# Attention and a two-layer network on one core: one 32-byte tile moves from behind the weights to ahead of them

## The chip, the cores and the metric

The kernel runs on one core of a Trainium2 chip. The metric is the device time of one execution in microseconds (us). The profile is of one execution, taken by the hardware profiler. TensorE (PE) multiplies matrices, and its weight loads are listed apart as PEld; VectorE is DVE, ScalarE is ACT, GpSimd is POOL, and SyncE (SP) issues the DMAs.

## What is computed

Attention with a block-causal mask (blocks of 64) over 8 batches, 8 heads, 576 positions and a head size of 64; then a network on the 4608 tokens of 512 features:

```python
scores = scale * np.matmul(q, k.transpose(0, 1, 3, 2))
scores = np.where(block_i >= block_j, scores, -1e9)
attn = softmax(scores)
x = np.matmul(attn, v)            # heads side by side: 4608 x 512
h = x @ w_in                      # 512 x 2048
g = np.maximum(0.01 * h, h)
out = g @ w_out                   # 2048 x 512
```

The large products are taken in a 4-byte type (fp32r). To keep precision, each operand of the large products is split into a high and a low part, and three of the four partial products are summed.

## The kernel before

**Order of the work.** Nothing is scheduled by hand. Each step is handed to a planner (class Plan) with the engines that may do it, a rank and a cost in ns; the planner plays the engines through and writes out one fixed order. Its costs depend on sizes alone, not on addresses.

**Stages.** The weights come in as 64-bit numbers, in 64 pieces, and are turned into high and low parts (wih, wil, woh, wol) during the first part of the run. Batches 0 and 1 go through attention with TensorE transposes, the later ones with VectorE transposes and a way through DRAM (line 703, line 720). As soon as 256 tokens of attention output are there (a chunk; 18 in all), the network runs on them, interleaved with the attention of later heads.

**The first product** (line 805). For each pair of 128-wide columns of w_in, twelve multiplications go into one accumulator of p_h: four slices of the 512 features, and for each the terms xh by wih, xl by wih and xh by wil. The stationary operand (the weight load) is a 128x128 block of wih or wil, 512 bytes per partition; the moving operand is 256 columns of xh or xl, 1024 bytes per partition.

**The second product** (line 824). After the activation (line 812) and its split into gh and gl, six multiplications go into each of two accumulators p_o. Here the stationary operand is a 128x128 block of gh or gl, and the moving operand is 512 columns of woh or wol, 2048 bytes per partition. Over the run there are 288 groups of twelve into p_h, and 288 groups of six into p_o.

**Where tiles lie.** A pool hands out its tiles in the order of their creation, each rounded up to 32 bytes per partition. 384 bytes lie ahead of the first tile (a scratch area of 256 and four constants of 32). The big tiles are whole multiples of 256 bytes, so a tile's place in a 512-byte line follows from what was created before it:

| tiles, in order of creation | bytes per partition, each | byte of the 512-byte line, before |
|---|---|---|
| wih, wil, woh, wol | 32768 | 384 |
| pth | 7168 | 384 |
| prow0_0 to prow0_4 | 512 to 2560 | 384 |
| qk_in0 | 4608 | 384 |
| qs0, qs1, kh0, kh1, kl0, kl1 | 2304 | 384, 128 in turn |
| vs | 2560 | 384 |
| nm0, nm1, sums0, sums1, rec0, rec1 | 32 (20 used) | 384, 416, 448, 480, 0, 32 |
| xr0 | 9216 | 64 |
| g, gh0, gh1, gl0, gl1, xh, xl, ob | 2048 or 4096 | 64 |
| pools of the stages: raw, val, ptf, later xr1, ptl, v_stage, ptm, turn | various | 64 or 320 |

nm holds the negated row maxima of the softmax (line 505 writes, line 514 reads), one small tile for even heads and one for odd ones.

Of the kernel before, what the change touches and what calls it, by code (L numbers as in the profile page):

```python
# [9 lines left out]
F32 = mybir.dt.float32  # L10
# [7 lines left out]
P = 128  # L18
# [3 lines left out]
NT = 5  # L22
# [204 lines left out]
def attention_ffn(ctx: ExitStack, tc: tile.TileContext, qk: bass.AP, v: bass.AP, w_in: bass.AP, w_out: bass.AP, out: bass.AP):  # L227
# [33 lines left out]
    def fixed(shape, dt, name, n=None, pool=const):  # L261
        if n is None:
            return pool.tile(shape, dt, name=name)
        return [pool.tile(shape, dt, name=f"{name}{i}") for i in range(n)]
# [3 lines left out]
    def identity(pool):  # L268
        one = fixed([P, P], F32, "ident", None, pool)
        make_identity(nc, one)  # L270
        return one

    wih = fixed([P, ND, DFF], F32R, "wih")
    wil = fixed([P, ND, DFF], F32R, "wil")
    woh = fixed([P, NF, DM], F32R, "woh")
# [24 lines left out]
    kh = fixed([P, S], F32R, "kh", 2)  # L300
    kl = fixed([P, S], F32R, "kl", 2)
    vs = fixed([P, NT, 2 * D], F32R, "vs")
    nm = fixed([P, NT], F32, "nm", 2)
    sums = fixed([P, NT], F32, "sums", 2)
    rec = fixed([P, NT], F32, "rec", 2)
    for y in range(2):
# [605 lines left out]
```

## Time and profile before

| | |
|---|---|
| median of 3 runs | 1120.84 us (1120.43 to 1126.4) |
| the profiled execution, its own time | 1119.52 us |
| its span, first to last instruction | 1117.7 us |
| TensorE busy, granted clock | 97%, 0.997 |
| weight loads busy | 87% |
| VectorE, ScalarE, GpSimd busy | 68%, 63%, 43% |
| DMA | 148 GB/s over the span |

A row of groups gives line, engine, operation, names, shapes and count, then busy time, the mean of one in ns, and the idle time of the engine before it with what ended it. Multiplications are pipelined: one that is listed with 280 ns is followed by the next after less than half of that, so the pace is read from the starts, or from the chain of waits, which lists pieces as start, length and count.

### The profile page before, as it was taken

Reading aid. Unit: us, or ns where it says so; the run is one execution under the profiler, and the core shown is the slowest. Engines: PE = TensorE matmul, PEld = TensorE weight load, DVE = VectorE, ACT = ScalarE, POOL = GpSimd, SP = SyncE. Lnnn points to the kernel's source line nnn. Section 1 sums busy time; section 2 is a strip of 40 time slices with the busy share of each in tenths; the row PEclk is TensorE's granted clock in tenths of the full one; section 3 lists DMA queues with packets and bytes.
Section 4 is the critical chain, followed back from the end, with each engine's and each line's share of the span. In section 5 each row is a group of like instructions: output and inputs, shape, how many; then the busy total and the mean of one; then the engine's idle time right before and its main releaser. Section 6 shows DMA issues by size and latency. Waiting matters only on the chain.

```text
span 1117.7 us, 20595 instructions
## 1 busy us (share of the span) xinstructions
PE 1083.7 (97%) x6896; PEld 971.3 (87%) x6896; DVE 762.2 (68%) x2115; ACT 708.3 (63%) x1696; POOL 475.5 (43%) x501
## 2 busy tenths in 40 slices
PE   5799999999999999999999999999999999999998
PEld 4578788888889989999999998999989998999997
DVE  6998978879878777877666678787877776400000
ACT  7998767767777766655655566676677765322222
POOL 3444244545544444433443345455444445422221
PEclk9999999999999999999999999999999999999999
DMA  7766421157766656564445456656676655200000
GB/s 235 231 201 198 133 95 61 61 173 208 199 198 189 201 170 201 176 170 147 128 151 148 128 171 185 203 171 203 176 205 185 194 156 160 59 20 19 1 20 19
DMA packets 96810, 166.24 MB, mean 149 GB/s; under 512 B 10176, under 2 KB 79808, under 8 KB 96704
## 3 DMA queue, kind: packets, MB, share of 16 engines
q1 hardware_dynamic: 96704, 164.93, 50.0%
q8 instruction: 54, 0.88, 0.3%
q14 instruction: 52, 0.43, 0.1%
HBM read 111.41 MB, written 53.48 MB: 148 GB/s over the span
## 4 chain that ended last, share of the span: by engine, by line
PE 69%; DVE 16%; ACT 6%; DMA 4%; issue 2%; SPq 1%; POOL 0%; ACTq 0%; DVEq 0%; POOLq 0%
PE p_h L805 27%; PE p_o L824 27%; PE p_t L641 6%; PE p_s L487 6%; DVE nm L505 4%; ACT prow L514 4%; DVE turn L703 2%; DVE qs L464 2%; DMA way<-turn 2%; DMA ptm<-way 2%; PE p_t L568 2%; PE p_s L481 1%; DVE p_s L498 1%; DVE ptl L253 1%; SPq L720 1%
## 5 line engine op out<-in xcount | busy, mean ns | idle before, releaser
L805 PE MATMUL p_h<-xh,wih 128*128 128x256 f32 x1152 | 327.0, 284 | 1.6 <-DVE xh L244 1.6
L805 PE MATMUL p_h<-xl,wih 128*128 128x256 f32 x1152 | 323.1, 280 | 1.0 <-DVE xl L253 0.9
L805 PE MATMUL p_h<-xh,wil 128*128 128x256 f32 x1152 | 322.5, 280 | 0.0
L254 POOL TENSOR_TENSOR gl<-g,gh 128x512 fp32r<-128x512 f32 x110 | 149.4, 1359 | 368.2 <-ACT gh L243 317.7
L805 PEld LDWEIGHTS p_h<-xl,wih 128*128 128x128 f32 x1152 | 218.6, 190 | 11.6 <-DVE xl L253 1.4
L805 PEld LDWEIGHTS p_h<-xh,wih 128*128 128x128 f32 x1152 | 217.9, 189 | 11.8 <-DVE xh L244 1.8
L805 PEld LDWEIGHTS p_h<-xh,wil 128*128 128x128 f32 x1152 | 219.4, 190 | 0.0
L514 ACT ACTIVATE prow<-p_s,nm 128x192 f32<-128x192 f32 (+4 forms) x308 | 160.0, 525 | 74.1 <-DVE nm L505 73.4
L812 ACT ACTIVATE g<-p_h 128x512 f32<-128x512 f32 x144 | 86.0, 597 | 174.6 <-PE p_h L805 168.4
L824 PE MATMUL p_o<-woh,gh 128*128 128x512 f32 x576 | 183.1, 399 | 0.0
L824 PE MATMUL p_o<-wol,gh 128*128 128x512 f32 x576 | 179.7, 393 | 0.0
L824 PE MATMUL p_o<-woh,gl 128*128 128x512 f32 x576 | 179.1, 392 | 0.0
L703 DVE STREAM_TRANSPOSE turn<-prow 128x384 f32<-128x384 f32 (+3 forms) x384 | 143.9, 401 | 33.2 <-POOL prow L542 24.0
L542 POOL TENSOR_SCALAR prow<-prow,rec 128x320 f32<-128x320 f32 (+4 forms) x142 | 77.3, 557 | 148.7 <-DVE rec L529 106.7
L505 DVE TENSOR_REDUCE nm<-p_s 128x1 f32<-128x192 f32 (+4 forms) x308 | 137.4, 480 | 3.3
L824 PEld LDWEIGHTS p_o<-woh,gl 128*128 128x128 f32 x576 | 108.2, 188 | 24.8
L824 PEld LDWEIGHTS p_o<-wol,gh 128*128 128x128 f32 x576 | 108.2, 188 | 24.4
L544 ACT ACTIVATE prow<-prow,rec 128x192 f32<-128x192 f32 (+4 forms) x124 | 75.5, 614 | 48.6 <-DVE rec L529 48.4
L243 ACT CAST gh<-g 128x512 fp32r<-128x512 f32 x139 | 86.1, 620 | 22.0 <-PE p_o L824 20.5
L254 POOL TENSOR_TENSOR ptl<-ptm,pth 128x448 fp32r<-128x448 f32 x83 | 97.6, 1193 | 3.6 <-ACT pth L243 3.6
L243 ACT CAST pth<-ptm 128x448 fp32r<-128x448 f32 x191 | 94.4, 564 | 5.4 <-DMA ptm<-way 4.9
L824 PEld LDWEIGHTS p_o<-woh,gh 128*128 128x128 f32 x576 | 90.9, 188 | 3.6 <-issue 0.4
(81 smaller groups left out, 1655.0 us busy)
## 6 DMA issues: line engine op xcount, KB each, us to landing
way<-turn SPq DMA_DIRECT2D x192, 224.0 KB, 3.0
ptm<-way SPq DMA_DIRECT2D x192, 224.0 KB, 4.3
qk_in<-in_qk SPq DMA_DIRECT2D x56, 576.0 KB, 3.8
v_stage<-in_v SPq DMA_DIRECT2D x56, 160.0 KB, 2.3
out<-ob SPq DMA_DIRECT2D x35, 256.0 KB, 2.5
raw<-in_w_in SPq DMA_DIRECT2D x32, 256.0 KB, 3.3
raw<-in_w_out SPq DMA_DIRECT2D x32, 256.0 KB, 3.4
qk_in<-in_qk SPq DMA_DIRECT2D x8, 320.0 KB, 3.6
```

Of the source, the lines that this page charges most:

```text
L243: one = lambda: nc.scalar.copy(dst(), src())
L254: ("POOL", pool2(n), lambda: nc.gpsimd.tensor_sub(dst(), one(), two())),
L487: go = lambda ap=ap, cols=cols, kk=kk, k0=k0, k1=k1, first=first, last=last: nc.tensor.matmul(ap, qs[z][:, cols], kk[:, k0:k1], start=firs ...
L505: [("DVE", dve(kw[t]), lambda t=t, ap=ap, flat=flat: nc.vector.tensor_reduce(nm[z][: qn[t], t : t + 1], ap[: qn[t]], axis=AX.X if flat els ...
L514: nc.scalar.activation(o, ap[: qn[t]], AF.Exp, bias=nm[z][: qn[t], t : t + 1], scale=1.0, accum_out=sums[z][: qn[t], t : t + 1])
L542: ("POOL", pool1(kw[t]), lambda: nc.gpsimd.tensor_scalar(p(), p(), by, 1.0, op0=ALU.mult, op1=ALU.mult)),
L544: ("ACT", act(kw[t], True), lambda: nc.scalar.mul(p(), p(), by)),
L641: nc.tensor.matmul(to, vs[:, j, :], src, start=start, stop=stop)
L703: nc.vector.transpose(dst, src.rearrange("p (s b i) -> p s b i", b=4, i=32))
L805: nc.tensor.matmul(hh[:, i, :], w[:, d, f * P : (f + 1) * P], x[:, d, :], start=k == 0, stop=k == len(terms) - 1)
L812: add([("ACT", act(512), lambda: nc.scalar.activation(g, hh, AF.Prelu, alpha=0.01))], rank, [("h", z)], ["g"])
L824: nc.tensor.matmul(p_o[m], a[:, i, m * P : (m + 1) * P], w[:, 2 * u + i, :], start=u == 0 and k == 0, stop=u == NU - 1 and k == 5,)
```

## The change

The first of the two small tiles nm is created ahead of the weights and not behind vs. The second is created where both were.

```diff
+    nm = [fixed([P, NT], F32, "nm0")]
     wih = fixed([P, ND, DFF], F32R, "wih")
     wil = fixed([P, ND, DFF], F32R, "wil")
     woh = fixed([P, NF, DM], F32R, "woh")
...
     vs = fixed([P, NT, 2 * D], F32R, "vs")
-    nm = fixed([P, NT], F32, "nm", 2)
+    nm.append(fixed([P, NT], F32, "nm1"))
     sums = fixed([P, NT], F32, "sums", 2)
```

All tiles from wih to vs start 32 bytes further: 384 becomes 416, and 128 becomes 160. nm1 and all that follows it (sums, rec, xr0, g, gh, gl, xh, xl, ob and the stages' pools) stay where they were. The instructions and their order are the same.

## The prediction

> **What bounds the kernel now.** I read the page first, then stretches of the span, then the engine's waits, then the chain of waits.
>
> ```profile
> span 1117.7 us, 20595 instructions
> ...
> PE 1083.7 (97%) x6896; PEld 971.3 (87%) x6896; DVE 762.2 (68%) x2115; ACT 708.3 (63%) x1696; POOL 475.5 (43%) x501
> ...
> PEclk9999999999999999999999999999999999999999
> ```
>
> TensorE is busy for 97% of the span at a granted clock of nine tenths or more in every slice, and apart from its own weight loads no engine comes above 68%. An average hides stages, so I cut the span into stretches; the columns are the stretch, its length, then busy time and instructions of each engine.
>
> ```profile
> 0.00:100.00 100.00, 80.87 (x444) 61.89 (x445) 85.68 (x283) 86.79 (x253) 40.89 (x65) 1.00 0.72 219
> 100.00:400.00 300.00, 289.98 (x1852) 259.20 (x1853) 248.46 (x678) 217.96 (x531) 142.66 (x159) 0.99 0.52 155
> 400.00:800.00 400.00, 399.47 (x2586) 365.26 (x2585) 295.34 (x800) 258.53 (x604) 177.69 (x172) 1.00 0.58 168
> 800.00:1040.00 240.00, 239.49 (x1551) 218.49 (x1550) 130.79 (x355) 126.90 (x282) 97.37 (x92) 1.00 0.42 123
> ```
>
> Up to 100 us TensorE (the first pair of figures) is not the limit: ScalarE and VectorE are each busier. From 400 to 1040 us it is busy for 638.96 of 640 us. The view of waits, TensorE alone, from 400 us to the end, has one row:
>
> ```profile
> PE p_s L487 <- ACT prow L514: 1.0, 4, 0.3
> ```
>
> So for the last 717.7 us TensorE waits 1.0 us in all. There the time is the number of matrix multiplications times the pace at which they follow each other, and nothing else. The multiplications are in these rows (count, busy time, mean of one):
>
> ```profile
> L805 PE MATMUL p_h<-xh,wih 128*128 128x256 f32 x1152 | 327.0, 284 | 1.6 <-DVE xh L244 1.6
> L805 PE MATMUL p_h<-xl,wih 128*128 128x256 f32 x1152 | 323.1, 280 | 1.0 <-DVE xl L253 0.9
> L805 PE MATMUL p_h<-xh,wil 128*128 128x256 f32 x1152 | 322.5, 280 | 0.0
> ...
> L824 PE MATMUL p_o<-woh,gh 128*128 128x512 f32 x576 | 183.1, 399 | 0.0
> L824 PE MATMUL p_o<-wol,gh 128*128 128x512 f32 x576 | 179.7, 393 | 0.0
> L824 PE MATMUL p_o<-woh,gl 128*128 128x512 f32 x576 | 179.1, 392 | 0.0
> ```
>
> 3 x 1152 = 3456 multiplications into p_h are 288 groups of twelve, and 3 x 576 = 1728 into p_o are 288 groups of six. The means of 280 to 399 ns overlap one another, so they are not the pace. The pace is in the chain of waits, whose pieces run from the first start of a group to the first start of the next. From 400 us on its long pieces are:
>
> ```profile
> 747.09 5.54 PE p_o L824 x24
> 753.15 5.65 PE p_h L805 x48
> ...
> 978.85 5.46 PE p_h L805 x48
> 1107.07 6.88 PE p_o L824 x30
> ```
>
> Here is what the case turns on. The same 48 multiplications, of the same shapes from the same tiles, with no wait before any, take 5.65 us at one place and 5.46 us at another: 117.7 against 113.8 ns each. So two paces exist. Short pieces show the mixture, first at 930 us, then at 938 us:
>
> ```profile
> 930.12 1.38 PE p_h L805 x12
> 931.50 1.37 PE p_o L824 x6
> 932.87 1.39 PE p_h L805 x12
> ...
> 938.52 1.41 PE p_h L805 x12
> 939.93 1.39 PE p_o L824 x6
> ```
>
> And inside a group the pace can switch. These are the first, the sixth and the twelfth multiplication of one group, and the first of the next (start, duration):
>
> ```profile
> 1080.67 0.28 PE L805 MATMUL p_h<-xh,wih 128*128 128x256 f32 x1
> ...
> 1081.27 0.28 PE L805 MATMUL p_h<-xh,wil 128*128 128x256 f32 x1
> ...
> 1081.95 0.28 PE L805 MATMUL p_h<-xh,wil 128*128 128x256 f32 x1
> 1082.06 0.62 PE L824 MATMUL p_o<-woh,gh 128*128 128x512 f32 x2
> ```
>
> Five steps in 0.60 us are 120 ns each, the next seven in 0.79 us are 113 ns each. The weight loads run beside the multiplications (PEld, 87%), so two streams leave the on-chip memory at once: the 512 bytes of the next stationary block, and the 1024 or 2048 bytes of the moving operand.
>
> **The change part by part.** No instruction is added, removed or reordered: the planner's costs know no addresses, so the order written out is the same. What changes is where tiles start. Everything allocated between the old and the new place of the small tile moves up by 32 bytes, everything behind it stays. By the tiles' sizes, weights, pth, prow, the first q and k tiles and vs go from byte 384 (or 128) of a 512-byte line to 416 (or 160); xr, g, gh, gl, xh, xl and ob stay at byte 64.
>
> The small tiles themselves cost nothing: the first starts at byte 384 of a line before and after, the second at 416, and the instructions that write and read them are not moved in time.
>
> The loads of q and k land 32 bytes further. They are 3.8 us from issue to landing, and over the run all their readers together idle 1.0 us for them:
>
> ```profile
> qk_in<-in_qk SPq DMA_DIRECT2D x56, 576.0 KB, 3.8
> ...
>   DMA qk_in<-in_qk: 1.0, 3
> ```
>
> The cover is the lead of the load over its use; without it a load slower by a tenth would cost 0.4 us at each of those 3 places. I take 0, between -1 and +1 us.
>
> VectorE, ScalarE and GpSimd read and write moved tiles (prow, qs, kh, kl, vs, pth). The nearest rows compare a subtraction whose three tiles lie at byte 64 with one that mixes 384 with the later pools:
>
> ```profile
> L254 POOL TENSOR_TENSOR gl<-g,gh 128x512 fp32r<-128x512 f32 x110 | 149.4, 1359 | 368.2 <-ACT gh L243 317.7
> ...
> L254 POOL TENSOR_TENSOR ptl<-ptm,pth 128x448 fp32r<-128x448 f32 x83 | 97.6, 1193 | 3.6 <-ACT pth L243 3.6
> ```
>
> 1359 / 512 and 1193 / 448 are 2.65 and 2.66 ns per element: the place does not show. I take 0 here too. The cover from 400 us on is TensorE's own work. Before 100 us there is none: if these engines slowed by 1%, it would cost about 1 us.
>
> TensorE's two streams are the part that can move the time. In the first product the loaded block comes from the weights (384, then 416) and the moving operand from xh or xl (64). In the second it is the other way round. No tile of this size in the trace starts off a multiple of 64 bytes, so the price of 416 has no row, and I bound it by the paces seen. From below: all groups run at the fast pace. A p_h group takes 1.39 us in the typical piece and 5.46 / 4 = 1.365 us at the fast pace: 0.025 x 288 = 7.2 us. A p_o group takes about 1.38 (between 1.37 and 1.39) and at best 1.37: 0.01 x 288 = 2.9 us. Together 10.1 us. Of all multiplications 444 + 1852 = 2296 of 6896, a third, lie before 400 us, where other engines set part of the pace; I count half of that third as lost, so 10.1 x 0.835 = 8.4 us. From above: all groups run at the slow pace, 5.65 / 4 = 1.4125 us for p_h and 1.39 us for p_o: 0.0225 x 288 + 0.01 x 288 = 9.4 us, and with the same share 7.8 us. Further up lies the 120 ns step: twelve of these are 1.44 us, 0.05 x 288 = 14.4 us, with p_o 17.3, and 14.4 us after the share.
>
> Which value? The pace is not set by a wait, by the clock or by the busy engines, since the group above switches from 120 to 113 ns with the work unchanged. What remains is how the two streams stand to each other. Today both start on multiples of 64 bytes, and the starts 64 and 384 differ by 320, five times 64. The change sets them half of 64 apart. If the slow pace is two streams meeting at the same place in step, this is the shift that keeps them from it; I take the fast pace, -8.4 us. This is a hypothesis, and the weakest step of the sum. Against it: a stream of 512 bytes passes every position of a line, so another start may only move the place of meeting.
>
> The sum is made against the profiled execution: 1119.5 us, of which 1117.7 are its span and 1.8 lie around it. 1119.5 - 8.4 = 1111.1 us. The median of the runs shown, 1120.84, is 1.3 us above that execution, so the forecast as a median is 1112.
>
> **The rivals.** First, nothing that can be measured: the start of a stream does not matter, or groups that gain are balanced by groups that lose. For it: paces of 113.8 and 117.7 ns occur with unchanged addresses, so the address is not what chooses between them. Also for it: multiples of 64 as far apart as 64 and 384 serve as moving operand without another wait. That the tile would not shift anything belongs here too, though by the sizes it does. Time: 1120.8. The Trainium skill, "SBUF — State Buffer", section "Who interferes with whom", is on this side: it gives TensorE two read ports of its own, one for the moving operand and one for the weight load, and has it never wait on anyone. By that rule the streams cannot collide, and the time stays. The trace does not settle it: it shows two paces without a wait, but not why.
>
> Second, slower: off the multiple of 64, the stream that starts at 416 touches one block more, the weight load ends later, and each multiplication into p_h starts a few ns later, so the group never falls to the fast pace. For it: the p_h steps are short (113 ns), so a weight load has little room beside one. Against it: p_o has twice the room, and there only its moving stream would pay. It decides as soon as more than half of the p_h groups run at 1.41 us or more. Time: 1120.8 + 7.8 = 1128.6; at the 120 ns step throughout, 1135.
>
> **How the numbers follow.** The forecast has 0.40, no change 0.35, slower 0.25. About 0.5%, 5.6 us, is what a measurement of this kernel can tell from no change, so the forecast's 8.4 us and the rival's 7.8 us both lie beyond it. Chances: faster 0.40, same 0.35, slower 0.25. The forecast's own range is 1108 to 1115. Cases of both signs hold much of the chance, so the range reaches to both. Below, the whole distance between the slow and the fast pieces, 72 x (5.65 - 5.46) = 13.7 us for p_h and 0.02 x 288 = 5.8 us for p_o, 19.5 us, is the most that I take a gain to be: 1101. Above, 1130 takes in the slower rival's 1128.6 and leaves out the 120 ns step throughout. About 0.05 lies below and 0.12 above.
>
> **What would show it.** Right: counts and order are unchanged, TensorE still waits about 1 us after 400 us, p_h pieces of twelve come near 1.365 us and of 48 near 5.46, and p_o pieces near 1.37. No change: the same mixture of 1.38, 1.39 and 1.41. Slower: p_h pieces at 1.41 or above throughout. The forecast is wrong in its reason if the time falls while these pieces keep their length, for then it came from the first 400 us; and if the time moves through the waits of another engine, the cost of zero given to those was wrong.

## The result, and the profile after

The changed kernel takes 1131.04 us (median of 5 runs, 1128.04 to 1135.18) against 1120.84: a ratio of 1.0088, with a 95% interval of 1.0058 to 1.0117. Of the five runs of the kernel before that belong to this comparison, one, at 1326.78 us, was slow and is not in the ratio, which is over fast runs. The changed kernel is slower, the forecast was faster, and the time lies just above the range. The profiled execution took 1129.98 us. Its page, and from the view by stretches the two between 100 and 800 us:

```profile
span 1128.2 us, 20595 instructions
...
PE 1094.6 (97%) x6896; PEld 977.6 (87%) x6896; DVE 761.3 (67%) x2115; ACT 708.6 (63%) x1696; POOL 475.1 (42%) x501
...
PEclk9999999999999999999999999999999999999999
```

```profile
100.00:400.00 300.00, 289.53 (x1837) 258.60 (x1837) 245.67 (x673) 217.09 (x528) 141.57 (x158) 0.99 0.52 154
400.00:800.00 400.00, 399.80 (x2561) 363.88 (x2560) 293.18 (x792) 254.79 (x592) 176.33 (x171) 1.00 0.57 166
```

The same 6896 multiplications, the same clock, and 10.9 us more busy time on TensorE (1094.6 against 1083.7), about as much as the span grew (10.5 us). VectorE, ScalarE and GpSimd are busy as long as before to within 1 us. Between 400 and 800 us TensorE is as full as before and gets through 2561 multiplications where it got through 2586. From 400 us on its view of waits has no row at all now. So nothing waits longer; the pace is lower. The groups of both products:

```profile
L806 PE MATMUL p_h<-xl,wih 128*128 128x256 f32 x1152 | 324.7, 282 | 1.0 <-DVE xl L253 0.9
L806 PE MATMUL p_h<-xh,wil 128*128 128x256 f32 x1152 | 324.5, 282 | 0.0
...
L825 PE MATMUL p_o<-woh,gh 128*128 128x512 f32 x576 | 185.1, 403 | 0.0
L825 PE MATMUL p_o<-wol,gh 128*128 128x512 f32 x576 | 181.4, 396 | 0.0
```

The chain of waits near the end, where TensorE runs nothing but the two products, before and then after (start, length, count):

```profile
1084.98 1.37 PE p_o L824 x6
1086.36 1.39 PE p_h L805 x12
1087.75 1.37 PE p_o L824 x6
1089.12 1.39 PE p_h L805 x12
```

```profile
1084.95 1.42 PE p_h L806 x12
1086.37 1.40 PE p_o L825 x6
1087.77 1.42 PE p_h L806 x12
1089.19 1.40 PE p_o L825 x6
```

Each kind of group is 0.03 us longer. The fast pace is gone from the long pieces too; this one took 5.46 us before:

```profile
986.34 5.70 PE p_h L806 x48
```

And inside a group there is no switch from 120 to 113 ns any more. First, sixth and twelfth multiplication, and the first of the next group:

```profile
1081.97 0.28 PE L806 MATMUL p_h<-xh,wih 128*128 128x256 f32 x1
...
1082.56 0.28 PE L806 MATMUL p_h<-xh,wil 128*128 128x256 f32 x1
...
1083.27 0.28 PE L806 MATMUL p_h<-xh,wil 128*128 128x256 f32 x1
1083.39 0.63 PE L825 MATMUL p_o<-woh,gh 128*128 128x512 f32 x2
```

0.59 us for five steps, 0.83 us for seven: 118 and 119 ns. It is so throughout: of the steps from one multiplication of a p_h group to the next after 400 us, 921 of 2335 are shorter than 115 ns before the change and 8 of 2346 after it.

For all that follows I use one measure: the mean length of a group from its first start to the first start of the next group, over the 210 or so groups of each kind after 400 us, worked out from all their starts in the trace (shorter pieces such as those above are single values of it). Before: p_h 1.400, p_o 1.385 us. After: 1.418 and 1.404. With 212 groups of each kind after 400 us, (0.018 + 0.019) x 212 = 7.8 us. By the starts of the same multiplications, the changed kernel is 2.2 us behind at 400 us and 10.5 us at the end, so it loses 8.3 us after 400 us, and the two products explain nearly all of that. What the first 2.2 us are is taken up further down.

### The profile page after: what moved, and what is told of

It reads as the page before. It is cut to its first block, busy times and chain, and to the rows that moved or that the text cites. A ratio compares the mean times of both kernels' runs of the same rounds, so it can differ in the third digit from the quotient of the medians.

```text
span 1128.2 us, 20595 instructions
## 1 busy us (share of the span) xinstructions
PE 1094.6 (97%) x6896; PEld 977.6 (87%) x6896; DVE 761.3 (67%) x2115; ACT 708.6 (63%) x1696; POOL 475.1 (42%) x501
## 4 chain that ended last, share of the span: by engine, by line
PE 66%; DVE 18%; ACT 6%; DMA 5%; issue 2%; SPq 1%; POOL 1%; ACTq 0%; DVEq 0%; POOLq 0%
PE p_h L806 25%; PE p_o L825 25%; PE p_t L642 5%; PE p_s L488 5%; ACT prow L515 4%; DVE nm L506 4%; DVE turn L704 3%; DMA way<-turn 2%; DVE qs L465 2%; PE p_t L569 2%; PE p_s L482 2%; PE p_t L629 1%; DMA qk_in<-in_qk 1%; DVE ptl L253 1%; SPq L721 1%
```

## The experiments

By **distance** I mean the byte of a weight tile's start in its 512-byte line less that of the activation tile with which it is multiplied, modulo 512: 384 - 64 = 320 before, 352 in the changed kernel. A pad is a tile of 32 bytes or more that nothing uses. No kernel leaves out any work. Times are ratios to the kernel before on the same chip.

**Both sides moved.** (Here and below, only the lines that differ and some around them are printed; ... stands for lines between.)

```diff
+    fixed([P, 8], F32, "pad")
     wih = fixed([P, ND, DFF], F32R, "wih")
```

> Every tile from wih to the end lies 32 bytes further than in the kernel before: weights at byte 416, inputs and activations at 96, so the two streams of a multiplication stand to each other as before. Theory A (it is the distance between the streams, modulo 64 bytes, that sets the pace): back to the pace of the kernel before, late groups of twelve into p_h 1.40 us, groups of six into p_o 1.385 us, about 1121 us. Theory B (a stream that starts off a multiple of 64 bytes is slower by itself): both streams of both products are off, so at least as slow as the changed kernel, 1131 us or more, p_h 1.42 and p_o 1.40 or above.

1.0003 (0.9981 to 1.0026), p_h 1.400, p_o 1.385 us. The chain near the end reads as before the change:

```profile
1080.81 1.37 PE p_o L825 x6
1082.18 1.39 PE p_h L806 x12
```

Here the weights lie at byte 416 as in the changed kernel, and it costs nothing. A start off a multiple of 64 is therefore no cost in itself: theory B falls.

**Only the activations moved**, by a pad of 32 bytes ahead of xr.

> Weights stay at byte 384, and xr, g, gh, gl, xh, xl, ob and the stages' pools move from 64 to 96. Theory A: the streams stand 288 bytes apart, off a multiple of 64 as in the changed kernel, so about 1131 us, p_h 1.42 and p_o 1.40. Theory B: now p_h has its moving stream off and p_o its weight load; if only a moving stream pays, p_h pays and p_o doesn't, about 1126 us; if only a weight load pays, the other way round, about 1126 us; if both pay, 1131 us.

1.0089 (1.0056 to 1.0122), p_h 1.423, p_o 1.397 us:

```profile
1080.24 1.39 PE p_o L825 x6
1081.62 1.42 PE p_h L806 x12
```

The weights have not moved, and the time is that of the changed kernel. So it is the distance between the moved and the unmoved tiles that counts. This pad also moves xr and the stages' pools; x_16 below leaves xr where it was, and wo_g_32_again moves the pools by 32 bytes at an unchanged time.

**One pair of weights moved, or the attention tiles alone.** Each time the small tiles nm are put elsewhere, as here for w_in_32; for w_out_32 they stand ahead of woh and of pth, for attn_32 the first stands ahead of pth.

```diff
+    nm = [fixed([P, NT], F32, "nm0")]
     wih = fixed([P, ND, DFF], F32R, "wih")
     wil = fixed([P, ND, DFF], F32R, "wil")
+    nm.append(fixed([P, NT], F32, "nm1"))
     woh = fixed([P, NF, DM], F32R, "woh")
...
-    nm = fixed([P, NT], F32, "nm", 2)
```

> Only wih and wil lie at byte 416; woh, wol and the attention tiles lie at 448, a multiple of 64, activations at 64. Theories A and B: only p_h pays, late groups of twelve 1.42 us, groups of six into p_o 1.385 as before, 288 x 0.018 = 5.2 us, about 1126 us. Theory C (the moved attention tiles are what costs): 1121 us.

1.0053 (1.0036 to 1.0069), p_h 1.419, p_o 1.396. p_h as expected, p_o not: with woh at 448 its distance is 384, and the next group of runs shows that 384 is not free.

> Only woh and wol lie at byte 416; wih and wil stay at 384, the attention tiles lie at 448, activations at 64. Theories A and B: only p_o pays, late groups of six 1.404 us, groups of twelve into p_h 1.40 as before, 288 x 0.019 = 5.5 us, about 1126 us. Theory C: 1121 us. If one product's pace hangs on the state that the other leaves behind, p_h changes too though its tiles have not moved.

0.9996 (0.9977 to 1.0016), p_h 1.387, p_o 1.407:

```profile
1080.94 1.41 PE p_o L825 x6
1082.35 1.38 PE p_h L806 x12
```

p_o pays 0.022 us per group, as foreseen, but p_h gets 0.013 shorter with its own tiles where they were, and the time stays where 1126 us was expected. So where the tiles of p_o lie matters to p_h too.

> Only the attention tiles behind the weights (pth, prow, the first q and k tile, qs, kh, kl, vs) lie at byte 416 or 160; weights at 384, activations at 64. Theory A: the two network products keep their distances, so 1.400 and 1.385 us per late group and about 1121 us; at most 1 to 2 us more from the products of attention that mix moved and unmoved tiles. Theory C (the moved attention tiles cost): 1126 us or more.

0.9993 (0.9969 to 1.0017), p_h 1.402, p_o 1.385: theory C falls.

**Which distances?** If 64 bytes were the grain, the next run would change nothing (both tiles nm ahead of wih).

> Both small tiles nm lie ahead of the weights: weights and attention tiles at byte 448, activations at 64, so the streams stand 64 bytes further apart than before. Theory A (distance modulo 64 bytes): paces as before, late groups of twelve 1.400 us, of six 1.385, about 1121 us. Theory D (any other distance is worse, up to the whole line of 512 bytes): slower, like the changed kernel, about 1130 us.

1.0080 (1.0055 to 1.0106), p_h 1.435, p_o 1.396:

```profile
1081.32 1.39 PE p_o L825 x6
1082.71 1.43 PE p_h L806 x12
```

Theory A as I had put it, modulo 64, falls. In x_16 xh and xl are views that start 16 bytes inside a larger tile:

> Only xh and xl start 16 bytes off a multiple of 64 (byte 80 and 144 of their lines); weights at 384, g, gh and gl at 64. If 32 bytes is the grain (16 is rounded off or half as bad): p_h between 1.400 and 1.418 us, p_o 1.385, 1121 to 1126 us. If 64 bytes is the grain and every start off it is alike: p_h 1.418, p_o 1.385, about 1126 us.

1.0048 (1.0024 to 1.0071), p_h 1.430, p_o 1.387. Outside both expectations: p_h is worse than at 352. The view of xl starts at 144, so its distance is 240 and that of xh 304; the run mixes two distances and can't be put beside the others. But of the tiles that it moves (xh, xl, ob and the stages' pools) the two products read only xh and xl: p_h pays, and p_o, whose operands were not moved, stays. So for p_h it is the place of xh and xl against the weights that matters, and not that of xr.

Then four runs further off, with small tiles moved ahead of the weights (four of them for w_128, six for w_192) or a pad ahead of xr (128 and 160 bytes):

> Four small tiles lie ahead of the weights: weights and attention tiles at byte 0 of the line, activations at 64; a weight tile stands 448 bytes after an activation tile, modulo 512 (320 before, 352 in the changed kernel). Theory E (both products run best near 320, and the pace falls off with the distance from it: groups into p_h were 1.400 us at 320, 1.418 at 352 and 1.423 at 288, 1.435 at 384 and 1.437 at 256): 128 away, p_h 1.46 to 1.47 us, p_o 1.40 or more, 1140 us or more. Theory F (the pattern repeats every 128 bytes): as before, 1.400 and 1.385 us, 1121 us.

1.0084 (1.0060 to 1.0107), p_h 1.416, p_o 1.404.

> All six small tiles lie ahead of the weights: weights, attention tiles and activations all at byte 64, distance 0. Theory E: as far from 320 as can be (192), p_h 1.47 us or more, 1145 us or more. Theory F: like the distances 384 and 256, p_h 1.436 and p_o 1.396 us, 1130 us.

1.0087 (1.0061 to 1.0112), p_h 1.437, p_o 1.389.

> Weights at 384, activations at 192, distance 192. Theory E: 128 on the other side of 320, p_h 1.46 to 1.47 us, 1140 us or more. Theory F: as before, 1121 us.

1.0081 (1.0059 to 1.0102), p_h 1.416, p_o 1.404.

> Weights at 384, activations at 224, distance 160. Theory E: p_h 1.47 us or more, 1145 us or more. Theory F: like 288 (160 and 288 differ by 128): p_h 1.423 and p_o 1.397 us, about 1131 us.

1.0117 (1.0096 to 1.0139), p_h 1.441, p_o 1.403.

Theory E's 1140 us and more did not come, nor did theory F's return to 1121 us at 448 and 192. But 448 and 192 agree to the last digit in both products, and they are 256 apart. That made theory F', a period of 256, with three runs for it (three or five small tiles ahead of the weights; a pad of 96 bytes ahead of xr):

> Weights at byte 480, activations at 64, distance 416. Theory F' (period 256): the paces of distance 160, late groups of twelve into p_h 1.441 and of six into p_o 1.403 us, about 1133 us. Theory E' (no period): no figure follows; between its neighbours 384 (1.435 and 1.396) and 448 (1.416 and 1.404), about 1130 us.

1.0108 (1.0068 to 1.0148), p_h 1.441, p_o 1.403, to the last digit what a_160 gave; its p_h does not lie between its neighbours at 384 and 448. The two chains, a_160 first:

```profile
1081.59 1.40 PE p_o L825 x6
1082.99 1.44 PE p_h L806 x12
```

```profile
1081.14 1.40 PE p_o L825 x6
1082.54 1.44 PE p_h L806 x12
```

> Weights at byte 32, activations at 64, distance 480. Theory F': p_h and p_o alike, within 0.005 us, to those of distance 224. Theory E': slower than before, 1128 us or more, with no tie to distance 224.

1.0047 (1.0021 to 1.0073), p_h 1.407, p_o 1.401.

> Weights at byte 384, activations at 160, distance 224. Theory F': p_h and p_o within 0.005 us of those of distance 480, and nothing says that they are worse than before. Theory E': slower than before, 1128 us or more.

1.0046 (1.0021 to 1.0070), p_h 1.407, p_o 1.401: again alike. All kernels in which the weights lie at one byte of the line and the activations at one, so that both products have the same distance, with the groups in us:

| distance | modulo 256 | kernel | p_h | p_o | ratio |
|---|---|---|---|---|---|
| 0 | 0 | w_192 | 1.437 | 1.389 | 1.0087 |
| 288 | 32 | act_32 | 1.423 | 1.397 | 1.0089 |
| 320 | 64 | before; all_32; attn_32 | 1.400, 1.400, 1.402 | 1.385 in all three | 1; 1.0003; 0.9993 |
| 352 | 96 | the changed kernel | 1.418 | 1.404 | 1.0088 |
| 384 | 128 | w_64 | 1.435 | 1.396 | 1.0080 |
| 160, 416 | 160 | a_160, w_96 | 1.441, 1.441 | 1.403, 1.403 | 1.0117, 1.0108 |
| 192, 448 | 192 | a_128, w_128 | 1.416, 1.416 | 1.404, 1.404 | 1.0081, 1.0084 |
| 224, 480 | 224 | a_96, w_160 | 1.407, 1.407 | 1.401, 1.401 | 1.0046, 1.0047 |

The kernel before has the best of the eight places. In w_in_32, with p_h at 352 and p_o at 384, each product has the table's value for its own distance to 0.001 (1.419 and 1.396). That does not hold everywhere: in w_out_32 p_h has 1.387 at 320, and p_o 1.407 at 352.

**Does a change of product hand on a state?** Two tries to keep w_out_32's better p_h without its worse p_o, by moving g, gh and gl with woh and wol.

> woh, wol, g, gh and gl lie 32 bytes further (416 and 96); wih, wil, xh and xl keep their places modulo 64. Inside each product the distance is a multiple of 64 as before; only where one product follows the other do a load and a moving stream stand 32 apart. Theory A with the pace set inside a product alone: 1.400 and 1.385 us, 1121 us. Theory A with a state that is handed over at the change of product (as the p_h groups of the run with only woh and wol moved, 1.387 us, suggest): p_h 1.387 and p_o 1.385 us, 288 x 0.013 = 3.7 us less than before, about 1117 us.

1.0078 (1.0054 to 1.0102), p_h 1.437, p_o 1.392. The expectation went by places modulo 64. The second pad puts xh and xl at byte 128, so p_h's distance is 256, and 1.437 is the table's value for 0 modulo 256. In the second try xh and xl are created ahead of g and stay at 64:

```diff
+    xh = fixed([P, ND, CH], F32R, "xh")
+    xl = fixed([P, ND, CH], F32R, "xl")
+    fixed([P, 8], F32, "pad")
     g = fixed([P, 2, CH], F32, "g")
```

> woh and wol at byte 416, g, gh and gl at 96, wih and wil at 384, xh and xl at 64 (they are created ahead of g): both products keep the distance 320, and only at the change of product a weight load and a moving stream of the other product stand 288 or 352 apart. Pace set inside a product alone: 1.400 and 1.385 us, 1121 us. State handed over at the change: p_h 1.387 as in the run with only woh and wol moved, p_o 1.385, 288 x 0.013 = 3.7 us less, about 1117 us.

1.0003 (0.9983 to 1.0024), p_h 1.389, p_o 1.398:

```profile
1080.72 1.38 PE p_h L807 x12
1082.11 1.40 PE p_o L826 x6
```

With both distances at 320, p_h gains 0.011 us per group and p_o loses 0.013: the gain of one is given back by the other, and the expected 1117 us did not come. So the place of one product's tiles against the other's does matter, and no version here beats the kernel before. That a state is handed over at the change of product is argued, not shown.

## Why the prediction was wrong

**Right:** TensorE's pace sets the end, order and counts are unchanged, and two paces exist without a wait. The bound from above, all groups at the slow pace of before (1.4125 and 1.39 us), was close to what came (1.418 and 1.404). The zeros held: attn_32 shows nothing for the attention tiles. Idle time for the loads of q and k rose from 1.0 to 2.8 us over five places; in all_32 it is 2.6 us over five places at an unchanged time, so it costs nothing that can be measured:

```profile
  DMA qk_in<-in_qk: 2.8, 5
DMA to landing us min/median/max: 2.8/3.8/6.1
```

**The step that failed** is the choice between the bounds: "if the slow pace is two streams meeting at the same place in step, this is the shift that keeps them from it; I take the fast pace". That the two streams' places against each other matter was right (all_32 and act_32). That a multiple of 64 is where they meet was a guess, drawn from the one place that the trace had seen, and wrong twice: a shift by 64 changes the pace (w_64) and only one by 256 was seen to leave it, and 320, which is 64 modulo 256, is the best place and not a bad one. In place of 8.4 us less, the fast steps all but vanished and the time rose by 0.88% (0.58 to 1.17%), 9.9 us. The trace of the one layout, with its fast and its slow pace, did not say which way another place goes.

**One term mis-sized, and one that the pair can't settle.** p_o's slow end, 1.39 us, was too low against 1.404: 0.019 us per group where I had 0.010, or 2.6 us over 288 groups. p_h's term had the right size. Four of the 211 p_h groups of before end in a wait of TensorE for ScalarE, the row of waits in the prediction, and take 1.80 to 1.86 us; without these four the means are 1.392 us before and 1.414 after, 0.022 apart where I had 0.0225.

I took half of the third before 400 us as hidden. The 2.2 us that the changed kernel is behind at 400 us decide nothing, because executions differ by more than that there: all_32 is 1.4 us ahead of the kernel before, and w_128, whose granted clock was 0.91 in the first 100 us, 5.2 us behind. The times of all 17 changed kernels say more. The sum of both products' losses per group, times 288 groups, lies above the measured interval in seven of them (a_160: 0.059 x 288 = 17 us against 10.8 to 15.6), and times the 212 groups after 400 us in one, by 0.1 us. The best fit is about 220 groups, an estimate from these ratios and their intervals; my share of 0.835 was 240. So before 400 us the groups lose less, or most of what they lose does not reach the end; that other engines set part of the pace there is the likely reason, not shown. With 220 groups of 0.037 us the slower rival stands at 1120.8 + 8.1 = 1129 us. That the time lies 1 us above the range is within the interval; that the sign was wrong is not.

**The rivals.** No change fell. For it stood that both paces occur with unchanged addresses; but the layout sets how often the fast one comes (921 of 2335 steps before, 8 of 2346 after). The Trainium skill's rule in "SBUF — State Buffer", "Who interferes with whom", that TensorE's two read ports are independent and that it never waits on anyone, would have left the time as it was. The runs disagree: with no semaphore wait, p_h groups take 1.400 to 1.441 us as the places of the two operands change; whether the two ports themselves collide, no run shows. Slower came true in sign and nearly in size (7.8 us against 9.9), but by luck: its mechanism, a load that touches one block more when it starts off a multiple of 64, is refuted by all_32. I also read the chain's pieces as running from start to start; they are placed by ends (a group that starts at 1081.97 stands in the chain at 1082.13), though their lengths agree.

**What stays open:** why the pace depends on the distance with a period of 256 bytes. That the weight load and the moving operand read the same part of the memory at one time is argued, not shown. So is the way in which one product's tiles act on the other's pace. In steps of 32 bytes, the distances 32, 64, 96 and 128 were not run, nor 256 for p_o, and steps below 32 bytes only in the mixed x_16.

## What to carry to other kernels

Where TensorE runs without waits, the places of the two operands against each other are a parameter of their own: moving the weights alone or the activations alone by 32 bytes cost 0.9% here, moving both cost nothing. The loss per group came out in the time when it was multiplied by the groups of the stages in which TensorE alone sets the pace, not by all of them. Read the pace from start to start, group by group, after each change of layout, and check that a change meant for something else has not moved a weight tile against its activations. When a trace has seen only one place, give both signs the same chance.

## What the runs showed of the hardware that was not expected

Two layouts whose distances differ by 256 bytes ran with the same pace to 0.001 us per group, three times for both products (160 and 416, 192 and 448, 224 and 480) and once for p_h alone (0 and 256). Over the eight places seen, p_h varies by 2.9% (1.400 to 1.441 us) and p_o by 1.4% (1.385 to 1.404), and the worst place costs 1.2% of the time (1.0117, 1.0096 to 1.0139).
